# A gated mix of softmax attention and linear attention on one core: four score banks for the exponentials, part of the feature softmax on GpSimd, 482 tiles on VectorE

## The chip, the core and the metric

The kernel runs on one core of a Trainium2 chip. A core has five engines, each with its own instruction queue that is worked strictly in order: TensorE (PE, with its weight loads shown as PEld), VectorE (DVE), ScalarE (ACT), GpSimd (POOL) and SyncE (SP, which here only starts DMAs). They share the on-chip memory SBUF (128 partitions). TensorE writes its products to PSUM, eight banks of 128 x 512 float32, which VectorE and ScalarE read. The engines wait for one another by semaphores.

The metric is the device time of one execution in microseconds (us). The kernel before takes 772.43 us in the median of 3 runs (772.12 to 772.61).

## The reference

There are 2048 tokens of width 512, 32 heads of 16. Branch A is softmax attention; branch B is linear attention whose features are two softmaxes over 16 numbers each; a sigmoid gate per token mixes the two. Both branches read the same `x`.

```
scores = einsum("bhqd,bhkd->bhqk", q, k) * (Dh ** -0.5)      # A: 32 heads x 2048 x 2048
o = einsum("bhqk,bhkd->bhqd", softmax(scores), v) ... @ wo
pq = einsum("bhsd,hdf->bhsf", q, w_phi); pk likewise          # B
phi = concatenate([softmax(p), softmax(-p)], axis=-1)         # for pq and for pk
kv = einsum("bhsf,bhsd->bhfd", phi_k, v);  z = einsum("bhsf->bhf", phi_k)
o = einsum("bhqf,bhfd->bhqd", phi_q, kv) / (einsum("bhqf,bhf->bhq", phi_q, z) + 1e-6) ... @ wo
out = g * a + (1 - g) * b
```

## The kernel before

**Tiles.** Branch A is cut into 2048 tiles ("units") of 128 keys x 512 queries for one head: four units with the same keys and queries and four different heads make a pack, 16 packs make a group (4 heads, 512 queries, all 2048 keys), and there are 32 groups, so 512 packs. A unit's scores are one TensorE matmul of 32 contraction rows (`_scores`, L931); the four strips of 32 rows of the array can work side by side, and the strip of unit u is u modulo 4. A unit's exponentials are made in one of two ways.

- On ScalarE: 1596 units. Their scores go into a ring of five PSUM banks (`NRING`), in groups of alternately three and two units (`GROUPS`). One TensorE step `qk` (`_qk`) writes a group, one ScalarE instruction (`_exp`, L978) reads it and writes bfloat16 exponentials into a ring of 25 SBUF slots (`ET`, `NSLOT`). Step `qk` k waits for exponential k-2, since that one frees its banks, and must be done when exponential k-1 ends if ScalarE is not to wait.
- On VectorE: 452 units, `NUMS` of them in each group, spread evenly. `_vector_batch` takes four at a time: each unit's scores (`vqk`) go into a bank of the pool, VectorE turns them into the bits of a bfloat16 number (`v_bits`, L847), and two instructions a batch add constants to the bits (`v_step`, L864, of 2048 and 4096 elements); the four tiles that come of it are summed by TensorE into the same accumulator (`pvx`).

TensorE then multiplies with the values (`_values`, L1034), four column strips side by side: one step `pv` a pack for ScalarE's units and `pvx` steps for VectorE's. A group gathers in one PSUM bank (4 x 17 rows: 16 values and the sum). `_norm` ends a group: a transpose on VectorE (L1055), the reciprocal of the sums, the product (L1067, on POOL) and, once for two groups, a transpose back on VectorE (L1072, `n_back`), which yields `onTA`.

**PSUM.** Banks 0 to 4 are the ring. Banks 5 to 7 are a pool (`free_banks`) for the accumulators, the `vqk` scores, all projections, and branch B.

**Branch B.** `_b_fuse` multiplies `w_phi` into the projection weights once (L1128, copied out by VectorE at L1133). Then, for 8 pairs of token tiles of keys and later 8 pairs of queries, `_b_pair` projects, copies out of PSUM (L1160), negates (L1179), takes the maximum as a tree (L1181, L1182), subtracts (L1184), takes the exponential on ScalarE (L1187, 128 x 2048), sums as a tree (L1189, L1190, L1192), takes the reciprocal (L1200) and multiplies (L1194): both softmaxes at once, all but the exponential on VectorE. Keys meet the values in `_b_kv` (L1211) and are summed on VectorE. A query tile is transposed by a DMA (L1243, `phiT`), multiplied (`_b_num`, L1260), normalized on VectorE (L1266 to L1270), transposed by a DMA (L1276) and projected together with branch A in `_out`.

**The order.** Nothing on the engines is in the order in which the code is written. `Plan.order` plays the whole kernel through with a cost for every operation and writes down each engine's order; the engines then follow it with semaphores. Due times count in packs (`QDUE`, `K0`, `SK`, `Q0`, `SQ`, `NDUE`). `_late` refuses a TensorE operation that by the planner's costs would make the next `qk` late. Where TensorE has room, the planner puts in products with zeros (`_fill`, L1041) or idle products (L950). A `vqk` may be placed beside a `qk` that leaves its strip free (`_beside`).

The lines that the text below uses most, with `_qk` and `_exp`:

```
NRING = 5
GROUPS = (3, 2)
deps=self.qks[-1:] + ([self.exps[k - 2]] if k >= 2 else ...
self.ET[:, a % NS:a % NS + n, cols], self.ps[:, a % NR:a % NR + n, cols], ACT.Exp, scale=SCALE
```

## Time and profile before

The profiled execution took 772.22 us; the span from its first to its last instruction is 770.2 us, and the granted TensorE clock was 1.0.

| engine | busy, us | share of the span |
|---|---|---|
| PE | 747.0 | 97% |
| ACT | 755.1 | 98% |
| DVE | 725.3 | 94% |
| POOL | 57.9 | 8% |

Busy time is the union of the records of an engine. The record of an instruction reaches from its start to the end of its last write, and the next one of the same engine can start before that: two records in a row overlap by about 0.2 us on ScalarE and by about 0.08 us on VectorE. So an engine can show no idle time and still start its next instruction late; the distance from start to start tells that. A group of the profile is a line of the code, an engine, an operation and a shape, with its count, its busy sum, the mean of one and the idle time before it.

### The profile page before, as it was taken

The page shows a single profiled execution, that of the slowest core. Times are in us where ns is not written, and L with a number is a line of the kernel's source. Part 1 is how long each engine was busy: PE and PEld are TensorE (multiplying, and loading weights), DVE is VectorE, ACT ScalarE, POOL GpSimd, SP SyncE. Part 2 cuts the span into 40 slices and gives each one's busy share as a digit, 9 for nine tenths or more (in the row PEclk, how much of TensorE's full clock was granted, in tenths as well). Part 3 has the DMA queues.
Part 4 walks back from the last instruction along what each step waited for, and adds up shares of the span by engine and source line. Part 5 has one row for each costly group of instructions (what it writes and reads, how often), then busy time and mean ns, then how long its engine had stood idle before and what let it go on. Part 6 is the DMA issues. An engine that isn't in the chain of part 4 may idle for free.

```text
span 770.2 us, 16369 instructions
## 1 busy us (share of the span) xinstructions
PE 747.0 (97%) x7126; PEld 231.5 (30%) x7126; DVE 725.3 (94%) x1207; ACT 755.1 (98%) x663; POOL 57.9 (8%) x73
## 2 busy tenths in 40 slices
PE   8999999999999999999999999999999999999998
PEld 4333333322322232222232223222323232322222
DVE  4789999999999999999999999999999999999994
ACT  6999999999999999999999999999999999999996
POOL 3200102000010100001001010000010101010000
PEclk9999999999999999999999999999999999999999
DMA  9510000000000000000111010102001110100000
GB/s 233 124 29 1 2 1 2 1 1 2 1 1 2 1 2 1 1 2 1 29 28 29 21 35 15 42 9 49 8 9 36 32 31 16 35 9 2 1 2 28
DMA packets 46456, 16.79 MB, mean 22 GB/s; under 512 B 40752, under 2 KB 45872, under 8 KB 46384
## 3 DMA queue, kind: packets, MB, share of 16 engines
q1 hardware_dynamic: 44512, 14.97, 9.1%
q8 instruction: 55, 0.90, 0.5%
q10 hardware_dynamic: 1872, 0.79, 0.4%
q14 instruction: 17, 0.14, 0.1%
HBM read 4.21 MB, written 2.10 MB: 8 GB/s over the span
## 4 chain that ended last, share of the span: by engine, by line
ACT 87%; PE 7%; DVE 5%; DMA 1%; SPq 0%; issue 0%
ACT ET L978 83%; ACT bq L1187 4%; PE ps L931 2%; PE ps L1034 2%; PE ps L640 2%; DVE vs L847 2%; DVE vs L864 1%; DMA xT<-in_A_x_dram 1%; DVE WB L1133 0%; DVE bq L1184 0%; PE ps L1041 0%; DVE bq L1160 0%; DVE btree L1182 0%; PE ps L749 0%; DVE ghB L802 0%; SPq L515 0%
## 5 line engine op out<-in xcount | busy, mean ns | idle before, releaser
L978 ACT ACTIVATE ET<-ps 128x1024 bf16<-128x1024 f32 (+2 forms) x641 | 725.7, 1340 | 2.4 <-PE ps L931 2.4
L931 PE MATMUL ps<-qT,kT 32*128 32x512 bf16 (+1 forms) x2053 | 304.9, 383 | 12.8 <-ACT ET L978 8.2
L847 DVE TENSOR_SCALAR vs<-ps 128x512 uint16<-128x512 f32 x452 | 297.4, 681 | 13.6 <-PE ps L931 11.9
L864 DVE TENSOR_SCALAR vs<-vs 128x2048 uint16<-128x2048 uint16 x226 | 214.8, 955 | 0.8
L1034 PE MATMUL ps<-ET,V 128*32 128x512 bf16 x1596 | 196.7, 387 | 0.1
L1034 PE MATMUL ps<-vs,V 128*32 128x512 bf16 x1808 | 179.9, 384 | 2.9 <-DVE vs L864 2.7
L931 PEld LDWEIGHTS ps<-qT,kT 32*128 32x128 bf16 x2053 | 76.9, 91 | 261.0 <-ACT ET L978 187.1
L1034 PEld LDWEIGHTS ps<-ET,V 128*32 128x32 bf16 x1596 | 49.9, 94 | 92.6 <-issue 79.7
L1041 PE MATMUL ps<-kT,zero 128*32 128x512 bf16 x760 | 75.1, 383 | 0.0
L1034 PEld LDWEIGHTS ps<-vs,V 128*32 128x32 bf16 x1808 | 45.1, 95 | 67.7 <-issue 31.3
L640 PE MATMUL ps<-WB,xT 128*128 128x512 bf16 x192 | 56.7, 384 | 0.4 <-DVE WB L1133 0.4
L728 POOL TENSOR_SCALAR qT<-qtmp,mask 128x512 bf16<-128x512 bf16 x30 | 25.6, 865 | 311.2 <-DVE qtmp L723 311.2
L1067 POOL TENSOR_TENSOR T<-T,rinv 128x512 bf16<-128x512 f32 x15 | 16.5, 1102 | 296.7 <-DVE rinv L1064 296.7
L640 PE MATMUL ps<-xT,WA 128*128 128x512 bf16 x120 | 35.8, 384 | 0.0
L1187 ACT ACTIVATE bq<-bq 128x2048 bf16<-128x2048 bf16 x16 | 31.5, 1970 | 0.4 <-DVE bq L1184 0.3
L1055 DVE STREAM_TRANSPOSE T<-ps 128x512 f32<-128x512 f32 x32 | 22.7, 710 | 7.7 <-PE ps L1034 7.2
L1041 PEld LDWEIGHTS ps<-kT,zero 128*32 128x32 bf16 x760 | 19.4, 95 | 18.9 <-issue 13.7
L1160 DVE CAST bq<-ps 128x512 bf16<-128x512 f32 x32 | 21.7, 683 | 2.2 <-PE ps L640 2.2
L640 PEld LDWEIGHTS ps<-WB,xT 128*128 128x128 bf16 x192 | 14.1, 97 | 27.3 <-issue 16.4
L1184 DVE TENSOR_TENSOR bq<-bq,btree 128x2048 bf16<-128x2048 bf16 x16 | 19.8, 1240 | 0.1
L1194 DVE TENSOR_TENSOR bq<-bq,brec 128x2048 bf16<-128x2048 bf16 x16 | 19.6, 1224 | 0.0
L640 PE MATMUL ps<-WoA,onTA 128*128 128x512 bf16 x64 | 18.7, 382 | 0.0
(75 smaller groups left out, 341.2 us busy)
## 6 DMA issues: line engine op xcount, KB each, us to landing
WB<-in_B_wqkv_dram SPq DMA_DIRECT2D x1, 1536.0 KB, 8.7
out_dram<-WB SPq DMA_DIRECT2D x12, 128.0 KB, 1.7
WA<-in_A_wqkv_dram SPq DMA_DIRECT2D x2, 384.0 KB, 4.5
WoB<-in_B_wo_dram SPq DMA_DIRECT2D x1, 512.0 KB, 3.8
WoA<-in_A_wo_dram SPq DMA_DIRECT2D x1, 512.0 KB, 4.8
WA<-in_A_wqkv_dram ACTq DMA_DIRECT2D x2, 128.0 KB, 3.0
WA<-in_A_wqkv_dram ACTq DMA_DIRECT2D x1, 256.0 KB, 4.2
WA<-in_A_wqkv_dram SPq DMA_DIRECT2D x1, 256.0 KB, 5.0
```

The source lines that it names most:

```text
L640: return e.matmul(out, lhs, rhs, start=start, stop=stop)
L728: x = self.plan.op("POOL", lambda e, side=side: e.tensor_scalar(self.qT[:, s0 + side, :], tmp, self.mask[:, side:side + 1], 0.0, op0=ALU.m ...
L847: parts.append(op("DVE", lambda e, j=j, job=job: e.tensor_scalar(va[:, 0, j, :], self._bank(job), SCALE * LOG2E * 128.0, float(ORIGIN), op ...
L864: o = op("DVE", lambda e, k=k, src=src, dst=dst: e.tensor_scalar(dst, src, float(STEPS[k - 1]), None, op0=ALU.add), 0.16 + k * n * QCH * 0 ...
L931: return e.matmul(out[:, cols], self.kT[32 * i:32 * i + 32, cp, kt * TOK:(kt + 1) * TOK], self.qT[32 * i:32 * i + 32, s, cols], start=True ...
L978: o = plan.op("ACT", lambda e: e.activation(self.ET[:, a % NS:a % NS + n, cols], self.ps[:, a % NR:a % NR + n, cols], ACT.Exp, scale=SCALE ...
L1034: ins = e.matmul(self._bank(ot)[32 * i:32 * i + 32, :], v[:, v0:v0 + 32], tile, start=(kt == 0), stop=(kt == self.NT - 1), tile_position=( ...
L1041: ins = e.matmul(self._bank(ot)[32 * i:32 * i + 32, :], self.zero[:], self.kT[:, 0, 0:QCH], start=False, stop=False, tile_position=(0, 32 ...
L1055: t1 = op("DVE", lambda e: e.transpose(T1[:, side].rearrange("p b s -> p (b s)"), src()), 0.735, deps=last, writes=[b_T1[side]], name="n_t ...
L1160: [lambda e, b, k=k: e.tensor_copy(bq[:, k].rearrange("p (g s v) -> p g s v", g=8, s=2)[:, :, 0, :], b.rearrange("p (g v) -> p g v", g=8))],
L1184: + [("b_sub", two(2048), lambda e: e.tensor_tensor(x, x, spread(tree[:, :, 0]), ALU.subtract))],
L1187: op("ACT", lambda e: e.activation(flat, flat, ACT.Exp), 1.8, reads=[b], writes=[b], name="b_exp", prio=due + 1)
```

## The change

- The score ring has four banks and every group two units (`NRING = 4`, `GROUPS = (2, 2)`); the pool has four banks. The exponentials go into 22 slots. `NUMS` adds up to 482, so 1566 units stay on ScalarE.
- Branch B no longer normalizes both softmaxes. With S+ and S- the two sums of a head, only the second softmax's exponentials are multiplied, by S+/S- (`_b_ratio`), so that both carry the factor S+. For keys the factor 1/S+ goes to the values and to the columns of ones beside them, now four a block (`_b_v`, 68 columns where 65 were); for queries it cancels in the quotient, and the 1e-6 is multiplied by S+ (`r_eps`, `m_den`).
- Moved to POOL: the negation, the two smaller sums of the tree, the last sum, and the reciprocal, which becomes seven instructions on 128 elements: a guess from the bits and two Newton steps (`_reciprocal`).
- The transpose back of branch A (`n_back`) becomes DMAs for all but the last pair of groups: 16 small ones that reorder blocks into `T3` (`mix`), and one that transposes (`back`).
- The weights of `w_phi` are permuted as they stream into TensorE, so that the copy at L1133 is a plain one.
- The planner's costs, latencies, priorities and due times are other numbers, `_late` also guards the end of the kernel, and the last three `pv` go first. `PAIRS`, `P_M`, `P_REC` and `P_BMUL` are 0: the code under them is not used. So the order of nearly all instructions differs.

```diff
-        if k < 2 or k >= len(self.qks) or any(d.end is None for d in self.qks[k].deps):
+        if k >= len(self.qks) > 0:
+            x = self.exps[-1]
+            if self.last.end is not None or x.end is None and self.exps[-2].end is None:
+                return False
+            done = self.exps[-2].end + x.cost if x.end is None else x.end
+            return end > done + self.LAT["ACT"] + self.MORE["ACT", "PE"] - self.SWITCH + self.TAIL
+        if k < 2 or any(d.end is None for d in self.qks[k].deps):
...
-    NEAR = 0.2
-    SAME = 16
-    OPEN = 99
...
+    TAIL = 9.0
+    NEAR = 0.05
+    SAME = 100
+    OPEN = 2
+    HURRY, FREE = 20, 20
...
-    NRING = 5
-    GROUPS = (3, 2)
-    NSLOT = 25
+    NRING = 4
+    GROUPS = (2, 2)
+    NSLOT = 22
...
-    NA, NST, LEAD = 2, 2, 8
+    NA, NST, LEAD = 2, 2, 7
...
-    URGENT, AHEAD, SOON, REST = 5, -(1 << 30), 4, 6
-    QDUE, KDUE, VDUE = 24, 17, 8
-    P_Q, P_MUL, P_NEG = 1, 1, 0
...
+    URGENT, AHEAD, SOON, REST = 4, -(1 << 30), 4, 6
+    QDUE, KDUE, VDUE = 24, 17, 11
+    P_Q, P_MUL, P_NEG = 1, 1, 1
+    P_REC, P_SUM = 0, 4
+    P_BACK, RATIO, BV = 1, 1, 8
+    P_M, P_BMUL, CHUNKS = 0, 0, 2
     GDUE = 26
...
-    VMIN = 12
-    ALONE, EARLY = 9, 8
-    PVP = 8
...
+    VMIN = 8
+    FAST = 3
+    VSOON = -2
+    PADK = 8
+    LAST, FIRST_OUT, NEXT_OUT, DEP_OUT = 0, 8, 0, 2
+    ALONE, EARLY = 12, 6
+    PVP = 10
...
-    NUMS = (4, 10, 12, 14, 14, 14, 14, 14, 14, 14, 14, 14, 15, 14, 16, 14, 13, 14, 15, 14, 17, 14, 15, 15, 14, 14, 11, 15, 21, 16, 21, 12)
+    NUMS = (6, 10, 12, 14, 14, 16, 13, 15, 14, 17, 16, 13, 17, 15, 19, 16, 11, 18, 14, 17, 19, 14, 17, 14, 15, 20, 14, 20, 12, 16, 20, 14)
...
+        plan.last = o
+        if p >= self.NPACK - self.FAST:
+            o.prio = -1000
...
-        if side == 1:
+        if side == 1 and not alone and self.P_BACK:
+            self.b_T3.readers = self.b_T3.readers or list(self.b_wphi.readers)
+            parts = [lambda e, i=i, c=c: e.dma_start(
+                self.T3[32 * c:32 * c + 32, :, 32 * i:32 * i + 32],
+                T2[32 * i:32 * i + 32].rearrange("p (b c) f -> p c b f", c=4)[:, c]) for i in range(4) for c in range(4)]
+            self.dma("SP", f"mix{due}", parts, cost=11.0, reads=[b_T2], writes=[self.b_T3], prio=due, lat=1.5)
+            self.dma("SP", f"back{due}", lambda e: e.dma_start(dst.rearrange("p (b t) -> p b t", b=4),
+                                                               self.T3[:].rearrange("p b f -> p (b f)"), transpose=True),
+                     cost=1.3, reads=[self.b_T3], writes=[b_dst], prio=due, lat=1.7)
+        elif side == 1:
...
-    NDUE = 26
-    K0, SK, Q0, SQ = 34.0, 12.0, 214.0, 14.25
+    NDUE = 23
+    K0, SK, Q0, SQ = 30.0, 11.5, 214.0, 15.25
...
+            if self.RATIO:
+                slot = self._b_pair(1, t, due)
+                for k in range(2):
+                    self._b_v(t + k, due + self.BV + k)
+                self._b_kv(t, slot, due + self.BV + 7)
+                continue
...
-                                   self.wphi[:, cp, :], start=True, stop=True)
+                                   self.wphi[:, cp, :].rearrange("p (g i f) -> p g f i", g=2, i=4), start=True, stop=True)
...
-                self.WB[:, c, D * s:D * s + D].rearrange("p (g f i) -> p g i f", g=8, i=4),
-                self._bank(job).rearrange("p (g i f) -> p g i f", g=8, i=4)), 1.19, deps=[m],
+                self.WB[:, c, D * s:D * s + D], self._bank(job)), self.c_dve(512), deps=[m],
...
-        if t < 4:
-            self.b_VB[t].writers = [self.o_vbones]
+        at = self.VB[:, t % 4]
+        b = self.b_VB[t % 4]
+        if self.RATIO:
+            r = self.recs[:].rearrange("p (t g s i) -> p t g s i", t=2, g=8, s=2)[:, t % 2, :, 0, :]
+            ones = self.plan.op("POOL", lambda e: e.tensor_scalar(at[:, :, 64:68], r, 1.0, 0.0, op0=ALU.mult, op1=ALU.add),
+                                0.2, reads=[self.b_tree], deps=list(b.readers) + [self.o_vbones], name="r_col", prio=due)
+            evac = lambda e, bank: e.tensor_tensor(
+                at[:, :, 0:64].rearrange("p g (i d) -> p g i d", i=4), bank.rearrange("p (g i d) -> p g i d", g=8, i=4),
+                r[:, :, :, None].to_broadcast([P, 8, 4, DH]), ALU.mult)
+        else:
+            ones, evac = self.o_vbones, lambda e, bank: e.tensor_copy(at[:, :, 0:64], bank.rearrange("p (g v) -> p g v", g=8))
         self._proj(lambda c: self.xT[:, c, TOK * t:TOK * t + TOK], lambda c: self.WB[:, c, 2 * D:3 * D],
-                   [self.b_xT[t // 4], self.b_WB],
-                   [lambda e, b: e.tensor_copy(self.VB[:, t % 4, :, 0:64], b.rearrange("p (g v) -> p g v", g=8))],
-                   self.c_dve(512), due + 4, due - 3, "bv", [self.b_VB[t % 4]])
+                   [self.b_xT[t // 4], self.b_WB], [evac], self.c_dve(512), due + 4, due - 3, "bv", [b],
+                   beside=[self.b_tree] if self.RATIO else [], after=[ones] if self.RATIO else [])
+        b.writers.append(ones)
...
         chain([("b_neg", 0.16 + 1024 * 0.00027, lambda e: e.tensor_scalar(both[:, :, 1], both[:, :, 0], -1.0, 0.0,
-                                                                         op0=ALU.mult, op1=ALU.add)),
+                                                                         op0=ALU.mult, op1=ALU.add),
+                self.P_NEG * 1.1),
                ("b_max", two(1024), lambda e: e.tensor_tensor(tree, x[:, :, 0:8], x[:, :, 8:16], ALU.max))]
...
         chain([("b_sum", two(1024), lambda e: e.tensor_tensor(half, x[:, :, 0:8], x[:, :, 8:16], ALU.add))]
               + [("b_sum", two(128 * n), lambda e, n=n: e.tensor_tensor(half[:, :, 0:n], half[:, :, 0:n],
-                                                                       half[:, :, n:2 * n], ALU.add)) for n in (4, 2)]
-              + [("b_sum", 0.3, lambda e: e.tensor_tensor(last(self.bsum[:]), half[:, :, 0], half[:, :, 1], ALU.add)),
-                 ("b_rec", 0.96, self._b_rec),
-                 ("b_mul", two(2048), lambda e: e.tensor_tensor(x, x, spread(last(self.brec[:])), ALU.mult))],
+                                                                       half[:, :, n:2 * n], ALU.add),
+                  (n <= self.P_SUM) * (0.13 + 0.25 * n)) for n in (4, 2)]
+              + [("b_total", 0.3, lambda e: e.tensor_tensor(last(self.bsum[:]), half[:, :, 0], half[:, :, 1], ALU.add),
+                  (self.P_SUM > 0) * 0.38)],
               2, [b, self.b_tree])
+        if self.RATIO:
+            self._b_ratio(b, x, s, t0, due + 2)
+            return slot
...
+    def _b_ratio(self, b, x, s, t0, due):
+
+        do = lambda name, cost, fn, eng="POOL", **k: self.plan.op(eng, fn, cost, name=name, prio=due, **k)
+        halves = lambda a: a.rearrange("p (t g s i) -> p (t g) s i", t=2, g=8, s=2)
+        plus = halves(self.bsum[:])[:, :, 0, :]
+        both = [b, self.b_tree]
+        ratio = self.brec[:, 0:64].rearrange("p (g i) -> p g i", i=4)
+        self._reciprocal(self.bsum[:], self.guess[:], self.newton, self.recs[:], [self.b_guess[0]], both, due)
+        do("r_mul", 0.29, lambda e: e.tensor_tensor(ratio, plus, halves(self.recs[:])[:, :, 1, :], ALU.mult), writes=both)
...
+                do("r_eps", 0.22, lambda e, k=k, t=t: e.tensor_scalar(
+                    self.eps[:, t % 4].rearrange("p (g i) -> p g i", i=4), plus[:, 8 * k:8 * k + 8], 1e-6,
+                    self.ghB[:, t:t + 1], op0=ALU.mult, op1=ALU.mult), reads=both + [self.b_gB],
+                   writes=[self.b_eps[t % 4]])
+        y = x.rearrange("p (g s) f i -> p g s f i", s=2)[:, :, 1]
+        n = 16 // self.CHUNKS if self.P_BMUL > s else 16
+        done = []
+        for a in range(0, 16, n):
+            do("b_mul", 0.17 + 0.00188 * 64 * n if n < 16 else 0.16 + 1024 * 0.000522, lambda e, a=a: e.tensor_tensor(
+                y[:, a:a + n], y[:, a:a + n], ratio[:, a:a + n, None, :].to_broadcast([P, n, DH, 4]), ALU.mult),
+               "POOL" if n < 16 else "DVE", writes=both)
+
+    def _reciprocal(self, s, guess, tmp, out, reads, bufs, prio):
+
+        n = s.shape[-1]
+        high = lambda a: a.bitcast(U16).rearrange("p (n two) -> p n two", two=2)[:, :, 1]
+        t, r = tmp[:, 0, 0:n], tmp[:, 1, 0:n]
+        do = lambda name, cost, fn: self.plan.op("POOL", fn, cost, reads=reads, writes=bufs, name=name, prio=prio)
+        do("r_bits", 0.17 + 0.001 * n, lambda e: e.tensor_scalar(
+            high(guess), high(s), -1.0, float(0x7EE0), op0=ALU.mult, op1=ALU.add))
+        for x, y, by, plus in ((guess, r, -1.2011100358638287, 2.192845599791731), (r, out, -1.0, 2.0)):
+            do("r_mul", 0.17 + 0.0019 * n, lambda e, x=x: e.tensor_tensor(t, s, x, ALU.mult))
+            do("r_rest", 0.17 + 0.001 * n, lambda e, by=by, plus=plus: e.tensor_scalar(
+                t, t, by, plus, op0=ALU.mult, op1=ALU.add))
+            do("r_step", 0.17 + 0.0019 * n, lambda e, x=x, y=y: e.tensor_tensor(y, x, t, ALU.mult))
 
...
-            d = op("DVE", lambda e, view=view, r=r: e.tensor_scalar(
-                r, view()[:, :, 16], 1e-6, self.ghB[:, t:t + 1], op0=ALU.add, op1=ALU.mult), 0.22, reads=[self.b_gB],
-                deps=[m] + was, name="m_den", prio=due - 20)
+            if self.RATIO:
+                d = op("DVE", lambda e, view=view, r=r, hf=hf: e.scalar_tensor_tensor(
+                    out=r, in0=view()[:, :, 16], scalar=self.ghB[:, t:t + 1], in1=self.eps[:, tt, 16 * hf:16 * hf + 16],
+                    op0=ALU.mult, op1=ALU.add), 0.22, reads=[self.b_gB, self.b_eps[tt]], deps=[m] + was, name="m_den",
+                    prio=due - 20)
```

More of the change, by code (lines that the diff above doesn't have):

```diff
@@ L602, in _projections @@
             if j == 0:
-                for half, banks in enumerate(((3, 4), (None, None))):
+                for half, banks in enumerate(((3, 4) if self.NRING == 5 else (3, 2), (None, None))):
                     self._proj_k0(half, banks[0])
@@ L651, in _wide_kind, with _proj @@
         return dict(kind="col", strips=range(4)) if self.COLS else {}
-    def _proj(self, lhs, rhs, reads, evac, cost, due, rel, name, writes, n=512, bank=None, urgent=1 << 30):
+    def _proj(self, lhs, rhs, reads, evac, cost, due, rel, name, writes, n=512, bank=None, urgent=1 << 30, beside=(), after=()):
         op = self.plan.op
@@ L657, in _proj @@
         mm = None
-        war = [r for b in writes for r in b.readers]
+        war = [r for b in writes for r in b.readers] + list(after)
         for c in range(4):
@@ L839, in _vector_batch, with place @@
         n, step = len(units), (units[-1] - units[0]) / 12
-        parts, war = [], list(b_va.readers)
+        parts, war, twin = [], list(b_va.readers), {}
+        pairs = min(self.PAIRS if units[0] // (4 * NT) >= self.PAIR0 else 0, n // 2)
+        def place(j):
+            a, b = twin.get(j // 2, (None, None))
+            return j ^ 1 if a is not None and a.bank > b.bank else j
         for j, u in enumerate(units):
@@ new lines, in _b_pair @@
+        self._reciprocal(self.bsum[:], self.guess[:], self.newton, self.brec[:], [self.b_guess[0]], [b, self.b_tree], due + 2)
+        r = last(self.brec[:])[:, :, None, :]
+        if self.P_BMUL > s:
+            n = 32 // self.CHUNKS
+            done = [op("POOL", lambda e, a=a: e.tensor_tensor(x[:, a:a + n], x[:, a:a + n],
+                                                              r[:, a:a + n].to_broadcast([P, n, DH, 4]), ALU.mult),
+                       0.1 + 0.00188 * 64 * n, reads=[b, self.b_tree], deps=b.writers + self.b_tree.writers, name="b_mul",
+                       prio=due + 2) for a in range(0, 32, n)]
+            b.writers, b.readers = done, []
+        else:
+            chain([("b_mul", two(2048), lambda e: e.tensor_tensor(x, x, spread(last(self.brec[:])), ALU.mult))],
+                  2, [b, self.b_tree])
@@ L1314, in _out @@
             for x in first:
-                x.prio, x.rel = due, due - (6 if not final else 8 if tt < 2 else 0)
+                x.prio, x.rel = due, due - (6 if not final else self.FIRST_OUT if tt < 2 else self.NEXT_OUT)
                 x.deps += deps
+            if final:
+                due += self.LAST
+                for x in first:
+                    x.prio = due
             m = first[-1]
```

185 lines of the change are left out of this document (130 added, 55 removed).

## The prediction

> **What bounds the kernel now.** I read the page's busy sums and its chain first, then the groups with their shapes kept apart, the stretches of the chain, and ScalarE's and TensorE's instructions in order of time.
>
> ```profile
> PE 747.0 (97%) x7126; PEld 231.5 (30%) x7126; DVE 725.3 (94%) x1207; ACT 755.1 (98%) x663; POOL 57.9 (8%) x73
> ACT 87%; PE 7%; DVE 5%; DMA 1%; SPq 0%; issue 0%
> ```
>
> The chain that ends last is ScalarE for 87% of the span. PE's 97% says little, since its records overlap. The groups:
>
> ```profile
> L978 ACT ACTIVATE ET<-ps 128x1536 bf16<-128x1536 f32 x318 | 494.5, 1555 | 0.4 <-PE ps L931 0.3
> L978 ACT ACTIVATE ET<-ps 128x1024 bf16<-128x1024 f32 x318 | 360.8, 1134 | 1.5 <-PE ps L931 1.5
> L931 PE MATMUL ps<-qT,kT 32*128 32x512 bf16 x2043 | 303.8, 384 | 12.5 <-ACT ET L978 8.2 <-DVE vs L847 1.2
> L847 DVE TENSOR_SCALAR vs<-ps 128x512 uint16<-128x512 f32 x452 | 297.4, 681 | 13.6 <-PE ps L931 11.9
> L1034 PE MATMUL ps<-ET,V 128*32 128x512 bf16 x1596 | 196.7, 387 | 0.1
> L1034 PE MATMUL ps<-vs,V 128*32 128x512 bf16 x1808 | 179.9, 384 | 2.9 <-DVE vs L864 2.7
> L864 DVE TENSOR_SCALAR vs<-vs 128x4096 uint16<-128x4096 uint16 x113 | 138.6, 1228 | 0.3
> L864 DVE TENSOR_SCALAR vs<-vs 128x2048 uint16<-128x2048 uint16 x113 | 76.7, 683 | 0.5
> L1041 PE MATMUL ps<-kT,zero 128*32 128x512 bf16 x760 | 75.1, 383 | 0.0
> L1187 ACT ACTIVATE bq<-bq 128x2048 bf16<-128x2048 bf16 x16 | 31.5, 1970 | 0.4 <-DVE bq L1184 0.3
> ```
>
> Idle of 1.9 us ahead of 636 exponentials is not all the waiting: records overlap, so the starts must be read. ScalarE in order of time (start, length), from two places, and one stretch of the chain:
>
> ```profile
> 299.20 1.15 ACT L978 ACTIVATE ET<-ps 128x1024 bf16<-128x1024 f32 x1
> 300.10 2.03 ACT L1187 ACTIVATE bq<-bq 128x2048 bf16<-128x2048 bf16 x1
> ...
> 519.21 1.57 ACT L978 ACTIVATE ET<-ps 128x1536 bf16<-128x1536 f32 x1
> 520.54 2.03 ACT L1187 ACTIVATE bq<-bq 128x2048 bf16<-128x2048 bf16 x1
> ...
> 522.58 43.91 ACT ET L978 x39
> ```
>
> From start to start two tiles take 0.904 us (299.20 to 300.10, and the commonest distance in the trace), three 1.331 (519.21 to 520.54), the feature exponential 1.80. The slope is (1.331 - 0.904)/512 = 0.83 ns an element, so an instruction costs 0.05 us before its first element. Without waits those 39 (20 short, 19 long) take 43.37 us; they took 43.91. Over all starts in the trace, the excess is 7.0 us behind two-tile exponentials (312 steady ones, mean 22 ns, 58 late by 20 ns or more) and 1.9 us behind three-tile ones (mean 6 ns): 9.0 us hidden in a busy ScalarE.
>
> Where do those 7 us come from? One late start, TensorE and ScalarE in order of time:
>
> ```profile
> 536.74 3.92 ACT L978 ACTIVATE ET<-ps 128x1536 bf16<-128x1536 f32 x3
> ...
> 538.58 0.67 PE L931 MATMUL ps<-qT,kT 32*128 32x512 bf16 x5
> ...
> 539.21 9.14 ACT L978 ACTIVATE ET<-ps 128x1536 bf16<-128x1536 f32 x8
> ```
>
> From 536.74 to 539.21 is 2.47 where 2.235 were due. Score matmuls on different strips run together in 0.39 us; here five took 0.67, because a `vqk` held a strip of the three-tile group, whose last tile started 0.23 late. 28 of the 58 late starts behind two-tile exponentials are such split groups and hold 3.7 us; 30, with 3.0 us, are a `qk` behind too much other TensorE work.
>
> **The change part by part.** The sum is made against the profiled execution, 772.2 us (span 770.2 and 2.0 around it), 0.2 under the median.
>
> ScalarE's work. Before: 318 x (0.904 + 1.331) = 710.7. After: 2048 - 482 = 1566 units; four come in half-width instructions (4 x 0.48 = 1.9), 1562 in 781 pairs at 0.904 = 706.0, so 707.9 against 710.7 and the short first and last instructions' 2.9: **-5.7 us**. Thirty tiles fewer save 30 x 0.427 = 12.8; 145 more instructions give 7.3 back. This lies wholly on the path.
>
> ScalarE's waits. They cost 9.0 now. Every `qk` will have the short window of 0.904, which only each second one has now. Upper bound: 22 ns at each of 781, 17.4 us; lower: the 6 ns of the long window, 4.9 us. A two-tile group takes two strips, so a `vqk` finds a free one beside it and splits become rare; what stays are the 30 crowded ones and crumbs, 3.3 us in 312 windows, 10.6 ns. 781 x 10.6 ns = **8.3 us**. I take this since it is counted in the same window; it is -0.7 against now.
>
> TensorE. Same kind follows same kind 0.22 after; between row, column and full-width steps it is 0.31 to 0.32. A window of 0.904 holds a `qk` and two steps of one kind (0.32 + 0.22 + 0.31 = 0.85). To be placed: 512 `pv`, about 484 `pvx` (452 x 482/452 plus a last batch), and full-width work worth about 560 steps (456 of 512 columns, 128 of 256, 288 small ones of 0.03): 1556 steps in 783 windows, with room for about 100 more beside the sixteen exponentials of 1.80 (eight steps of 0.22 there instead of two). That fits at 93%, with the zero products (760 matmuls, 190 steps, 41 us) left out. Cost 0 if the `vqk` go beside; if not, below.
>
> VectorE. Off by mean durations: negation 6.6 (L1179), sums 11.2 and 4.5 (L1190, L1192), reciprocal, half the product, 15 of 16 transposes back, and L1133's plain copy (8 x (1.312 - 0.684) = 5.0):
>
> ```profile
> L1200 DVE RECIPROCAL brec<-bsum 128x128 f16<-128x128 f32 x16 | 15.1, 945 | 0.1
> L1194 DVE TENSOR_TENSOR bq<-bq,brec 128x2048 bf16<-128x2048 bf16 x16 | 19.6, 1224 | 0.0
> L1072 DVE STREAM_TRANSPOSE onTA<-T 128x512 bf16<-128x512 bf16 x16 | 11.2, 701 | 0.0
> ```
>
> 15.1 + (19.6 - 16 x 0.675) + 10.5: together 62 us. On: 30 x 0.681 + 8 x (0.683 + 1.228) = 35.7. Net -26 of 725, and the pool gains a bank. VectorE isn't the end of the chain, so I count 0; it keeps TensorE's waits on L847 and L864 (4.8 us in all) from growing.
>
> GpSimd. A pair's chain: negation 1.4 (two L728, 0.69 undisturbed), sums of 512 and 256 elements 1.1 and 0.6 and the last 0.4 (by L1067, 1.06 for 512), seven steps of about 0.3 (bounds 0.2, the 128x128 memset, and 1.06), ratio, eps or columns 0.8: 6.4 us, x16 = 102, POOL from 58 to 160 of 770. From exponential to feature it is 5.9 us where 3.8 were; pairs lie some 35 to 45 us apart, so it is covered. If not: `b_max` waits for `b_neg`, `b_mul` for the ratio, and behind them on VectorE stand `v_bits`, which free banks; and the value projection on TensorE waits for `r_col`, with `qk` behind it. Range 0 to 15 us, taken as 0, nearest to L1187's present wait of 0.3.
>
> What GpSimd costs VectorE shows in one place:
>
> ```profile
> 647.63 2.31 POOL L728 TENSOR_SCALAR qT<-qtmp,mask 128x512 bf16<-128x512 bf16 x2 [10.98 <-DVE qtmp L723]
> ...
> 648.04 2.98 DVE L864 TENSOR_SCALAR vs<-vs 128x2048 uint16<-128x2048 uint16 x3
> ```
>
> Two masks of 0.69 took 2.31, and three steps took 2.98 where 0.683 + 0.601 + 1.134 is 2.4. L864's long form is 1.22 alone and 1.46 in the mean of five that met POOL. The Trainium skill (Advanced Engine Details and Errata, VectorE Performance Modes) says GpSimd and VectorE's two-port modes block each other; the trace agrees, 1.22 against 1.46. Were all 102 us of new POOL time to meet such steps and each cost VectorE its full length, VectorE would lose 102 instead of winning 26, and would become the bound; by the row's 0.24 a meeting and with a third of the 224 new instructions (14 a pair) meeting one, it loses 18.
>
> DMA. `mix` is 16 issues on SP, 0.43 each by the weight loads at L578 (bound above: a transpose's 1.28), 7 to 20 us, then a transpose (2.4 to 3.2 to landing): some 12 us later than L1072, behind and ahead of phiT, onTB and the stores in SP's queue. Needed by `_out` 8 packs (12 us) after the last group of a block; a late one delays stores only. The last pair keeps VectorE's way: 0.
>
> Head and tail: the first exponential starts at 7.9, the last ends at 762.2, and the 8 us behind it are four transposes' worth of VectorE, the projection and the store, all kept. Slots 25 to 22 still lead by 11 exponentials, 10 us: 0.
>
> Sum: 772.2 - 5.7 - 0.7 = **766 us**. Own range 761 to 770: waits of 4.9 and of 12.
>
> **The rivals.** *TensorE becomes the bound* (slower). For it: 93% full, windows of mixed kind (0.32 + 0.32 + 0.31 = 0.95) are 0.05 late, a third step makes 1.06, 0.16 late. If one window in four is late by 0.08 on average, 783/4 x 0.08 = 15.7: **782 us**. Against: 41 us of zero products show spare time, and 197 `vqk` that now stand alone behind another score step, 0.24 each, can go beside. It decides from a mean lateness of 19 ns (18.8 x 781 = 14.7, with which the sum is 772.2). The Trainium skill (TensorEngine Tiling, Key Properties) says that a change of tiling mode drains TensorE; here 0.32 against 0.22, and 145 more groups with two changes each would be 29 us, 795 if none were covered.
>
> *GpSimd is late* (the meetings above). If `b_neg` is stretched as L728 was (0.69 to 1.65), each of 16 feature exponentials waits up to 0.95, 15 us; at two thirds 10: **776 us**. Against: 16 places only, 0.3 us of wait now.
>
> *It brings nothing*: splits go on and each window costs 22 ns, 757.5 + 17.4 = **775 us**, near no change; for it, the row as it stands.
>
> **How the numbers follow.** Chances: forecast 0.57, nothing gained 0.15 (half of it, with fewer splits, within 0.2%), TensorE 0.16, GpSimd 0.12. A measurement of this kernel tells a change from none at about 0.2%, 1.5 us. Faster 0.57, same 0.08, slower 0.07 + 0.16 + 0.12 = 0.35. The range reaches from 759, below the forecast's own, to 786, leaving out the worse half of the TensorE case and little else.
>
> **What would show it.** Right: two-tile exponentials 0.904 apart at the median, mean near 0.915, about 785 of them; hardly a `qk` of two passes; zero products far below 760; VectorE near 700 us busy, POOL near 160; L1187 waiting under 1 us in all. Wrong: L978's distance above 0.925, TensorE without zero products and `qk` late behind column steps, or L1187 behind L1184 by several us.

## The result, and the profile after

The changed kernel takes **781.64 us** in the median of 4 runs (780.35 to 783.90), the kernel before 772.45 us beside it (772.12 to 772.61): a ratio of 1.0123, with a 95% interval of 1.0099 to 1.0147. The forecast was 766 us and faster. The time lies inside the range of 759 to 786, on the wrong side of no change.

The page of the changed kernel, its busy sums, the granted clock in 40 slices of 19.5 us, and the chain that ended last:

```profile
PE 754.9 (97%) x7047; PEld 218.5 (28%) x7111; DVE 711.2 (91%) x1158; ACT 753.0 (97%) x807; POOL 208.9 (27%) x300
...
PEclk9995999999999999999999999999999999999999
...
ACT 74%; PE 19%; DVE 5%; DMA 1%; issue 1%
```

The span is 780.1 us of a profiled execution of 781.93. ScalarE's share of the chain has fallen from 87% to 74%, and TensorE's has risen from 7% to 19%. The line to see is the clock: in the fourth slice it is 5 tenths, where the kernel before had 9 (which stands for 90% or more) in all 40. The mean granted clock is 0.986, where 1 is full speed.

Its groups, with shapes kept apart (busy sum, mean ns of one, idle time before and what ended it):

```profile
L1041 ACT ACTIVATE ET<-ps 128x1024 bf16<-128x1024 f32 x781 | 723.2, 1168 | 13.0 <-PE ps L993 12.6 <-PE ps L1100 0.2
L1107 PE MATMUL ps<-kT,zero 128*32 128x512 bf16 x664 | 66.5, 384 | 0.0
L1216 PE MATMUL ps<-wphi,WT 128*128 128x128 bf16 x32 | 7.8, 394 | 0.2 <-issue 0.2
L1221 DVE CAST WB<-ps 128x512 bf16<-128x512 f32 x8 | 5.5, 690 | 1.3 <-PE ps L1216 1.2
```

and the answer of the kernel before to the third of them:

```profile
L1128 PE MATMUL ps<-wphi,WT 128*128 128x128 bf16 x32 | 3.2, 221 | 0.1
```

The exponentials are now L1041, the scores L993, the products of `w_phi` L1216 and their copy L1221. Idle time before the exponentials is 13.0 us, where the two shapes of before had 1.9 together. The 32 products of `w_phi` last 0.394 us each instead of 0.221. VectorE's copy of them has become the plain one that the forecast priced (0.690).

Where the 13.0 us lie is seen in stretches of 5 us of the changed kernel (length; busy time of PE, PEld, DVE, ACT and POOL, with the number of instructions; granted clock; DMA share; GB/s):

```profile
55.00:60.00 5.00, 4.84 (x37) 1.65 (x37) 4.57 (x7) 4.61 (x6) 0.00 (x0) 1.00 0.00 0
60.00:65.00 5.00, 5.00 (x24) 1.40 (x22) 4.15 (x6) 2.56 (x3) 0.00 (x0) 0.70 0.34 70
65.00:70.00 5.00, 4.67 (x15) 0.90 (x15) 1.17 (x2) 3.07 (x3) 0.00 (x0) 0.50 0.16 35
70.00:75.00 5.00, 5.00 (x22) 0.91 (x21) 1.67 (x3) 3.07 (x3) 0.00 (x0) 0.50 0.01 3
75.00:80.00 5.00, 4.84 (x27) 1.02 (x29) 1.59 (x3) 3.69 (x4) 0.00 (x0) 0.60 0.00 0
80.00:85.00 5.00, 5.00 (x42) 1.66 (x43) 3.18 (x5) 3.30 (x4) 0.00 (x0) 1.00 0.00 0
```

From 62 to 79 us the clock is at half, ScalarE works 3 us in 5, and PE shows as busy all the while. The order of time around the fall (start, length):

```profile
59.12 2.80 PE L1216 MATMUL ps<-wphi,WT 128*128 128x128 bf16 x12
61.85 0.52 PE L993 MATMUL ps<-qT,kT 32*128 32x512 bf16 x2
62.40 2.11 ACT L1041 ACTIVATE ET<-ps 128x1024 bf16<-128x1024 f32 x2 [1.89 <-PE ps L993]
...
70.06 1.02 ACT L1041 ACTIVATE ET<-ps 128x1024 bf16<-128x1024 f32 x1 [0.48 <-PE ps L993]
71.57 1.02 ACT L1041 ACTIVATE ET<-ps 128x1024 bf16<-128x1024 f32 x1 [0.48 <-PE ps L993]
```

Three things are to be seen. The twelve products stand 0.219 us apart ((2.80 - 0.394) / 11) and hold TensorE for 2.7 us; the next scores stand behind them, and an exponential waits 1.89 us. Right behind them the clock falls. And at half clock the exponentials come mostly 1.51 us apart instead of 0.904.

Read from the starts, as in the prediction, the waits behind two-tile exponentials add up to 24.6 us. 15.7 of these lie in the first 140 us, and 11 of them between 59 and 83 us. From 140 us on it is about 1 us in each 70 us, 12 to 15 ns a window.

### The profile page after: what moved, and what is told of

Its sections match the earlier page's. It is cut to its first block, busy times and chain, and to the rows that moved or that the text cites. A ratio compares the mean times of both kernels' runs of the same rounds, so it can differ in the third digit from the quotient of the medians.

```text
span 780.1 us, 16892 instructions
## 1 busy us (share of the span) xinstructions
PE 754.9 (97%) x7047; PEld 218.5 (28%) x7111; DVE 711.2 (91%) x1158; ACT 753.0 (97%) x807; POOL 208.9 (27%) x300
## 4 chain that ended last, share of the span: by engine, by line
ACT 74%; PE 19%; DVE 5%; DMA 1%; issue 1%
ACT ET L1041 71%; PE ps L993 6%; PE ps L1100 5%; PE ps L677 4%; ACT bq L1283 3%; PE ps L788 2%; DVE vs L900 2%; DVE vs L925 1%; PE ps L1216 1%; DMA xT<-in_A_x_dram 1%; DVE bq L1256 0%; DVE btree L1277 0%; DVE ghB L841 0%; PE ps L685 0%; PE ps L724 0%
## 5 line engine op out<-in xcount | busy, mean ns | idle before, releaser
L1041 ACT ACTIVATE ET<-ps 128x1024 bf16<-128x1024 f32 (+1 forms) x785 | 725.3, 1165 | 13.4 <-PE ps L993 13.0
L900 DVE TENSOR_SCALAR vs<-ps 128x512 uint16<-128x512 f32 x482 | 312.5, 682 | 25.0 <-PE ps L993 23.5
L993 PE MATMUL ps<-qT,kT 32*128 32x512 bf16 (+1 forms) x2052 | 317.2, 387 | 10.9 <-ACT ET L1041 5.9
L925 DVE TENSOR_SCALAR vs<-vs 128x2048 uint16<-128x2048 uint16 (+2 forms) x242 | 233.8, 976 | 1.2
L1100 PE MATMUL ps<-vs,V 128*32 128x512 bf16 x1928 | 211.3, 385 | 0.6 <-DVE vs L925 0.3
L1100 PE MATMUL ps<-ET,V 128*32 128x512 bf16 x1566 | 196.6, 390 | 0.3 <-DVE vs L900 0.2
L993 PEld LDWEIGHTS ps<-qT,kT 32*128 32x128 bf16 x2052 | 77.7, 91 | 317.7 <-ACT ET L1041 291.5
L1286 POOL TENSOR_TENSOR btree<-btree 128x512 f16<-128x512 f16 (+1 forms) x32 | 37.7, 1180 | 187.5 <-DVE btree L1285 186.5
L1100 PEld LDWEIGHTS ps<-ET,V 128*32 128x32 bf16 x1566 | 49.1, 94 | 82.4 <-issue 73.5
L1107 PE MATMUL ps<-kT,zero 128*32 128x512 bf16 x664 | 66.5, 384 | 0.0
L1100 PEld LDWEIGHTS ps<-vs,V 128*32 128x32 bf16 x1928 | 48.2, 95 | 51.2 <-issue 31.1
L1274 POOL TENSOR_SCALAR bq<-bq 128x1024 bf16<-128x1024 bf16 x16 | 20.3, 1266 | 138.3 <-DVE bq L1256 94.5
L677 PE MATMUL ps<-WB,xT 128*128 128x512 bf16 x169 | 51.9, 383 | 2.7 <-issue 2.2
L1283 ACT ACTIVATE bq<-bq 128x2048 bf16<-128x2048 bf16 x16 | 32.9, 2056 | 0.0
L805 POOL TENSOR_SCALAR V<-V 128x544 bf16<-128x544 bf16 x16 | 12.7, 793 | 30.3 <-DVE V L798 30.1
L1280 DVE TENSOR_TENSOR bq<-bq,btree 128x2048 bf16<-128x2048 bf16 x16 | 19.5, 1220 | 0.1
```

Source lines behind the costliest of these rows:

```text
L677: return e.matmul(out, lhs, rhs, start=start, stop=stop)
L900: bits = lambda e, to, src: e.tensor_scalar(to, src, SCALE * LOG2E * 128.0, float(ORIGIN), op0=ALU.mult, op1=ALU.add)
L925: o = op("DVE", lambda e, k=k, src=src, dst=dst: e.tensor_scalar(dst, src, float(STEPS[k - 1]), None, op0=ALU.add), 0.16 + k * n * QCH * 0 ...
L993: return e.matmul(out[:, cols], self.kT[32 * i:32 * i + 32, cp, kt * TOK:(kt + 1) * TOK], self.qT[32 * i:32 * i + 32, s, cols], start=True ...
L1041: o = plan.op("ACT", lambda e: e.activation(self.ET[:, a % NS:a % NS + n, cols], self.ps[:, a % NR:a % NR + n, cols], ACT.Exp, scale=SCALE ...
L1100: ins = e.matmul(self._bank(ot)[32 * i:32 * i + 32, :], v[:, v0:v0 + 32], tile, start=(kt == 0), stop=(kt == self.NT - 1), tile_position=( ...
```

## The experiments

The theory, formed from this trace: the loss is the permuted operand of L1216 alone. It acts in two ways: the products hold TensorE, and while they stream slowly the array is so empty that the clock is halved. Rivals: the new GpSimd work and the crowded windows of TensorE, as in the prediction; and, within the theory, that the hold alone is the loss and the clock only goes with it. "Waits" below are always the excess of the starts behind two-tile exponentials, which is 24.6 us in the changed kernel.

**1. The operand alone taken back.** The changed kernel in its own order of instructions, the products reading `w_phi` as it is stored, the permutation back in VectorE's copy.

```diff
-  self.wphi[:, cp, :].rearrange("p (g i f) -> p g f i", g=2, i=4), start=True, stop=True)
+  self.wphi[:, cp, :], start=True, stop=True)
...
-  self.WB[:, c, D * s:D * s + D], self._bank(job)), self.c_dve(512), deps=[m],
+  self.WB[:, c, D * s:D * s + D].rearrange("p (g f i) -> p g i f", g=8, i=4),
+  self._bank(job).rearrange("p (g i f) -> p g i f", g=8, i=4)), self.c_dve(512), deps=[m],
```

> The changed kernel, every engine's order kept, with only the products of w_phi as they were before: the moving operand in its stored order, the permutation back in VectorE's copy. Theory A (the permuted operand makes 32 small products four times as long, holds up score steps at 57 to 62 us and lets the clock fall to half for 17 us): those products 0.22 us long again, no half clock near 60 us, granted clock 0.995 or more, 766 to 770 us. Theory B (four banks and two-tile windows leave TensorE too little room, the clock only follows): still within 3 us of 781.6. Theory C (GpSimd's new work is late): also within 3 us of 781.6.

Measured: 771.75 us (10 runs), ratio 0.9987 (0.9978 to 0.9997). Ten of the 781.6 us are gone with one operand, while all GpSimd work and the ring of four stay. The groups of this kernel:

```profile
L1041 ACT ACTIVATE ET<-ps 128x1024 bf16<-128x1024 f32 x781 | 721.8, 1171 | 3.3 <-PE ps L993 2.7 <-PE ps L1100 0.2
L1221 DVE CAST WB<-ps 128x512 bf16<-128x512 f32 x8 | 9.8, 1303 | 0.0
L1216 PE MATMUL ps<-wphi,WT 128*128 128x128 bf16 x32 | 3.0, 221 | 0.4 <-issue 0.2
```

The waits are 14.0 us, and no slice shows half a clock. VectorE's copy is 1.30 again where the order was planned for a plain one, which may be why the time is 1.8 us above the expected range. So the operand is the cause. How much of the loss is hold and how much is clock, this run doesn't say.

**2. Held as long, with the array full.** The kernel of experiment 1 with each product issued four times into the same place.

```diff
-                for cp in range(4):
+                for cp in [x for x in range(4) for _ in range(4)]:
```

> As the run with the plain order, but each of the 32 small products of w_phi is issued four times, so that TensorE is held as long as by the permuted operand, with the array streaming all the while. A1 (the clock falls since the slow products leave the array nearly empty): no half clock near 60 us, 768 to 773 us, 3 us above the plain order at most. A2 (the clock falls since score steps are late and TensorE then waits for ScalarE): half clock near 60 us again, 778 to 784. Theories B and C: 779 to 784.

Measured: 773.29 us (10 runs), ratio 1.0015 (1.0004 to 1.0026), 0.3 above the range of A1 and 4.7 below that of A2; the waits are 16.5 us. Stretches of this kernel, in the columns of above:

```profile
55.00:60.00 5.00, 5.00 (x77) 3.84 (x75) 4.58 (x6) 3.43 (x4) 0.00 (x0) 1.00 0.01 3
60.00:65.00 5.00, 4.75 (x34) 1.47 (x33) 4.96 (x7) 4.33 (x5) 0.00 (x0) 1.00 0.51 105
65.00:70.00 5.00, 5.00 (x43) 1.24 (x41) 2.47 (x5) 5.00 (x7) 0.00 (x0) 1.00 0.00 0
```

TensorE is held as long as by the permuted operand, an exponential behind the products waits as long (1.94 us late at 60.7 us), and the clock stays full. So the hold alone does not bring the clock down; it takes the slow streaming. What is left to the changed kernel is 8.3 us.

**3. The operand alone put into the kernel before.** The kernel before in its own order, with the permuted operand and the plain copy.

> The kernel before, every engine's order kept, with only the permuted operand of the change (and the plain copy behind it). Theory A in its strong form: the products take 0.39 us, the clock falls to half between 45 and 65 us and the time is 780 to 786. In a weak form (here the 8 steps stand singly, 44 to 63 us, so the array stays busy around them): clock 1.0 and 774 to 777, the 5 us of added TensorE time partly covered. Theories B and C: 772 to 773, no effect.

Measured: 778.20 us (4 runs, 776.80 to 779.84), ratio 1.0074 (1.0054 to 1.0095), between the two forms expected. ScalarE's largest wait in this kernel and two of its stretches:

```profile
ACT ET L978 <- PE ps L931: 8.0, 15, 1.5
```

```profile
65.00:70.00 5.00, 4.67 (x27) 1.44 (x28) 3.01 (x6) 3.58 (x3) 0.00 (x0) 0.77 0.00 0
70.00:75.00 5.00, 5.00 (x19) 0.86 (x17) 1.54 (x4) 3.77 (x5) 0.00 (x0) 0.55 0.00 0
```

The clock falls here too, for 6.8 us from 67.7 on, without a ring of four and without GpSimd's new work. The four runs part by it: two with a mean clock of 0.996 took 779.5 and 779.8 us, two with 1.0 took 776.8 and 776.9. So even where the clock holds, the operand costs 4.6 us in this order (776.85 against 772.27 of the kernel before beside it). Alone it makes the old kernel slower, though it saves VectorE 4.2 us (9.7 to 5.5 in its copies).

**4. The planner told the true duration.** In the changed kernel the four products of a step are one operation of 4 x 0.22 us for the planner, and the order is made anew.

> The changed kernel with the permuted operand kept, but with 0.22 us a product in the planner's costs instead of 0.056, so that it places other work and the score steps around them by their true length; the whole order differs. Theory A: the score steps near 60 us are on time again, clock 0.995 or more, 767 to 772 us. Theories B and C: 778 to 784.

Measured: 807.42 us (4 runs), ratio 1.0454 (1.0421 to 1.0486), and not what the theory expected. The source view of L1216 (minimum, median, maximum of the length in ns, then first and last start) and the largest wait of this kernel:

```profile
L1216 PE MATMUL ps<-wphi,WT x32: 377/397/397, 162.1 to 183.0; 128*128 128x128 bf16 x32
```

```profile
ACT bq L1283 <- DVE bq L1280: 33.9, 2, 18.1
```

In the changed kernel the products start at 56.8 us, here at 162.1. A step of 0.88 us nearly fills a window of 0.904, so `_late`, as I read it, refuses it behind one score step after the other; when it comes at last, two feature exponentials wait 33.9 us together for their features, on the path, and the clock falls three times between 163 and 205 us. A true price in the planner was worse than a wrong one, since it was the price of a step too large to place.

**5. The same price in four steps.** As 4, but each product is an operation of its own of 0.22 us.

> The permuted operand is kept, with its true 0.22 us in the planner's costs, but each of the 32 products is a step of its own instead of four in one of 0.88. The order differs. If the run with the true cost was slow because a step of 0.88 fits no window of 0.904 beside a score step, so that the planner put it off to 162 us and ScalarE waited for the features: products between 54 and 100 us again, no wait of ScalarE on L1283's line above 2 us, clock 0.99 or more, 768 to 780 us (the order as a whole is another, untuned). If it was slow for another reason: above 790 us.

Measured: 784.72 us (4 runs), ratio 1.0151 (1.0131 to 1.0172), above the 768 to 780 expected. The products come from 55.4 to 105.5 us and the wait for L1280 is gone, so the reading of experiment 4 holds. The profiled execution, of 781.24 us, has a mean clock of 1.0; the three others had 0.991 to 0.993 and took 784.57 to 786.32 us. The new order also brought waits of its own, the two largest new ones of which on ScalarE are the gate's and one at the values:

```profile
ACT gh L833 <- DVE gh L830: 7.4, 1, 7.4
...
ACT ET L1041 <- PE ps L1100: 5.3, 1, 5.3
```

An order made with one number changed is another order. These two runs therefore say nothing on the operand's own price; the runs in a kept order do.

**6. Permuted once, by GpSimd.** The changed kernel in its order of instructions, with four small copies on GpSimd that write the permuted `w_phi` into a tile of its own; the products read that as it is stored, and VectorE's copy stays plain.

```diff
+        self.wphi2 = sb("wphi2", [P, 4, P], BF16)
+    def _permute(self, e):
+        for c in range(4):
+            ins = e.tensor_scalar(self.wphi2[:, c, :].rearrange("p (g f i) -> p g f i", g=2, i=4),
+                self.wphi[:, c, :].rearrange("p (g i f) -> p g f i", g=2, i=4), 1.0, 0.0, op0=ALU.mult, op1=ALU.add)
...
-  self.wphi[:, cp, :].rearrange("p (g i f) -> p g f i", g=2, i=4), start=True, stop=True)
+  self.wphi2[:, cp, :], start=True, stop=True)
```

> The changed kernel, every engine's order kept, but w_phi is permuted once, by four small GpSimd copies into a second tile at the start; the 32 products read it in stored order and VectorE's copy out stays the plain one, so that every step is as long as the planner has it. Theory A (the permuted operand is the whole loss, and the plain-order run still paid for VectorE's longer copies between 57 and 97 us): products 0.22 us long, clock 0.998 or more, ScalarE's waits near 10 us, 765 to 769 us, which is the forecast. Theory D (what the plain-order run still lost comes from elsewhere, GpSimd or the four banks): 770 to 773.

Measured: **768.20 us** in the median of 12 runs, ratio 0.9959 (0.9941 to 0.9976): faster than both kernels, and within the 765 to 769 of the theory. Nine of the runs lie between 767.84 and 769.91 us. Two took 773.95 and 774.07 with a mean clock of 0.991, and one 932.86 with 0.655, which the ratio leaves out (768.16 is the median without it); no trace of these three was kept, and their cause is open. The groups of this kernel:

```profile
L1041 ACT ACTIVATE ET<-ps 128x1024 bf16<-128x1024 f32 x781 | 720.9, 1177 | 1.6 <-PE ps L993 1.3 <-PE ps L1100 0.2
L1227 DVE CAST WB<-ps 128x512 bf16<-128x512 f32 x8 | 5.2, 678 | 0.0
L1222 PE MATMUL ps<-wphi,WT 128*128 128x128 bf16 x32 | 2.6, 220 | 0.2 <-issue 0.2
L1209 POOL TENSOR_SCALAR wphi<-wphi 128x128 bf16<-128x128 bf16 x4 | 1.5, 417 | 0.7 <-DMA wphi<-in_B_w_phi_dram 0.7
```

and its products in order of time:

```profile
56.70 0.84 PE L1222 MATMUL ps<-wphi,WT 128*128 128x128 bf16 x12
```

Twelve products take 0.84 us, 0.056 apart ((0.84 - 0.22) / 11), a quarter of the 0.219. The permutation costs GpSimd 1.5 us, once, at 28.4 us, and GpSimd has nothing else to do for 2.3 us behind it. In the profiled execution the clock is full throughout, and the waits are 11.5 us. Its chain shows 75% for ScalarE and 18% for TensorE, about as the changed kernel's, so the shift from 87% and 7% was not the loss. The 3.6 us by which this kernel is below experiment 1 go with VectorE's copy, which is plain here.

**7. Permuted once, and held all the same.** The kernel of experiment 6 with each product issued four times, as in 2.

> The kernel with w_phi permuted once into its own tile (768.2 us), with each of its 32 small products of w_phi issued four times into the same place, so that each holds TensorE about as long as the permuted operand did while the array goes on streaming. Same order of instructions, VectorE's plain copy kept. Theory (the clock falls because the array streams too little while the permuted operand is read, and the fall is the larger part of the loss): only the hold is paid, 769 to 773 us, granted clock 1.0 near 60 us, the waits within the exponentials' starts some 2 to 4 us more than the 11.5 us of the kernel with the permuted tile; what is left to the 781.6 us of the changed kernel, 9 to 12 us, is the half clock alone. Rival (the time for which TensorE is held is the loss, whatever the array does): 778 to 783 us.

Measured: 773.63 us (10 runs), ratio 1.0021 (1.0011 to 1.0031), 0.6 above the expected range and 4.4 below the rival's. A stretch of this kernel, and two rows of its order of time, one of PE's and one of ScalarE's:

```profile
55.00:60.00 5.00, 5.00 (x78) 3.88 (x75) 4.23 (x6) 3.11 (x4) 0.00 (x0) 1.00 0.01 3
...
57.13 2.85 PE L1222 MATMUL ps<-wphi,WT 128*128 128x128 bf16 x48
...
60.35 6.52 ACT L1041 ACTIVATE ET<-ps 128x1024 bf16<-128x1024 f32 x7 [1.82 <-PE ps L993]
```

The hold is 2.85 us, as in experiment 2, and the exponential behind it waits nearly as it did (1.82 us); the clock stays full, and seven exponentials follow without a pause, where the changed kernel's stood 1.5 us apart. The waits are 16.9 us, 5.4 more than in experiment 6, and the time is 5.4 us more. This takes the loss apart in one order of instructions: 768.2 without it, + 5.4 for the hold, + 8.0 for the half clock and what goes with it, 781.6.

**8. The ring of four alone.** The kernel before with four banks, groups of two and 24 slots, still 452 tiles on VectorE; a projection at the start moves from bank 4, which is gone, to bank 2.

```diff
-    NRING = 5
-    GROUPS = (3, 2)
-    NSLOT = 25
+    NRING = 4
+    GROUPS = (2, 2)
+    NSLOT = 24
```

> The kernel before with the ring of four banks and groups of two alone (24 slots; 452 tiles, VectorE and GpSimd as before); the order differs. ScalarE's own work: 796 x 0.904 + 1.9 = 721.5 against 713.6, so +7.9 us. If two-tile windows are late by about 10 ns each, as the forecast had it (waits 8 us): 778 to 782. If each is late by 22 ns as the two-tile windows of the kernel before (17 us): 786 to 790. If TensorE has no room (theory B): above 790, or a lower clock.

Measured: 785.81 us (4 runs), ratio 1.0171 (1.0157 to 1.0184), 13.4 us more, between what the two theories expected. By the prediction's own prices the work grows by 796 x 0.904 + 1.9 - 713.6 = 7.9 us; the waits grow from 9.0 to 15.7, 20 ns a window. One of them is a clock again, from 310.8 us for 3.4 us, and here TensorE had been idle for half of the 5 us ahead of it:

```profile
305.00:310.00 5.00, 2.44 (x27) 0.73 (x26) 5.00 (x8) 4.90 (x5) 0.00 (x0) 1.00 0.00 0
310.00:315.00 5.00, 5.00 (x45) 1.02 (x42) 4.11 (x7) 4.01 (x5) 0.00 (x0) 0.66 0.00 0
```

**9. The thirty tiles given back.** The kernel of experiment 6 with `NUMS` of the kernel before (452).

> As the run with w_phi permuted once, with the tile counts of the kernel before (452 instead of 482 on VectorE); the order differs. Thirty tiles more on ScalarE are 15 instructions of 0.904, 13.6 us. If ScalarE is the bound throughout: 12 to 16 us above the run with w_phi permuted once, 778 to 784. If TensorE bounds (theory B: fewer pvx steps and more zero products make room): less than 8 us above it.

Measured: 786.69 us (4 runs), ratio 1.0181 (1.0160 to 1.0202), 18.5 us more than with 482 tiles; 12 to 16 were expected. Two of its stretches:

```profile
305.00:310.00 5.00, 4.06 (x14) 0.85 (x14) 4.28 (x6) 3.71 (x4) 3.90 (x5) 0.69 0.00 0
310.00:315.00 5.00, 5.00 (x32) 0.88 (x31) 1.89 (x3) 3.21 (x4) 4.15 (x8) 0.50 0.08 8
```

The work of 30 tiles is 30 x 0.904 / 2 = 13.6 us on ScalarE, and the waits are 4.6 us more (16.1). Of these 16.1, 5.2 lie between 303 and 319 us: TensorE stood idle for 2.3 us up to 305.9, and from 306.9 to 317.1 the clock was at half. So what went beyond the tiles' work is about the size of that fall. Against experiment 8 (785.8) the rest of the change, the new feature softmax above all, shows no gain as long as VectorE gets no more tiles: its use is the time that it leaves VectorE for them. How a ring of five with 482 tiles would do was not tried.

## Why the prediction was wrong

The step that failed is the one on L1133's plain copy, "8 x (1.312 - 0.684) = 5.0", taken together with TensorE's "288 small ones of 0.03" and "Cost 0". The prediction booked what the permuted operand gives VectorE, and left the 32 products at the price of any small matmul, so that their cost on the path was nothing. The runs showed 13.4 us in its place (781.64 against 768.20 without the operand): 5.4 for the hold and 8.0 with the clock; no term of the prediction stood for either. The edit moves the permutation from VectorE's copy into TensorE's operand, and there it costs 0.219 us instead of 0.056 for each product: 32 x 0.163 = 5.2 us of TensorE. A stretch of 2.7 us, three windows long, was not hidden by a ring that is two groups ahead: the exponential behind it waited 1.9 us. To read it, the prediction needed the order of the operand's elements: in the new view neighbours lie 16 elements (32 bytes) apart. The Trainium skill (Advanced Engine Details and Errata, SBUF Cachelines) says that reads which hit another 16-byte line with each access pay for it. The traces agree, by a factor of four (0.219 against 0.056). No row of the kernel before showed such an operand on TensorE, so it should have been given bounds, as every unseen price.

Point by point:

- **ScalarE's work, -5.7: right.** 781 two-tile exponentials, 0.904 apart at the median; the first of them starts 0.7 us later than before (8.6) and the stretch behind the last is 0.6 longer (8.6).
- **ScalarE's waits, 8.3 us: wrong in the changed kernel, 24.6; nearly right without the operand, 11.5** (experiment 6: 15.1 ns in the mean, 10.6 forecast). The 2.2 us by which experiment 6 stands above the forecast's 766 are within this term's 3.2.
- **TensorE, "Cost 0 if the `vqk` go beside": right for the steady windows, wrong for one place.** From 140 us on the waits are 1 us in 70. The zero products are 664, "far below 760" was too much said: TensorE kept more room than thought.
- **The TensorE rival, 782 us, came out at the right number by another mechanism.** It put a mean lateness of 20 ns over all windows; the loss sits in one stretch some 25 us long. That the measured time agrees is luck and says nothing for it.
- **GpSimd late, 776 us: fell.** POOL was busy 208.9 us, not 160 (its instructions of 128 elements took 0.48 to 0.72 us each, taken as 0.3), and yet L1283 waited 0.0 us for its features, and the kernel of experiment 6 has the same POOL work in 768.2 us.
- **VectorE, "near 700", was 711**: in the changed kernel its step of 2048 elements took 0.714 in the mean and the one of 4096 took 1.244, against 0.683 and 1.228. The meetings with GpSimd are there, and small in sum (121 x 0.031 + 120 x 0.016 = 5.7 us): the 37 steps of 2048 elements that ran beside a GpSimd instruction took 0.780 in the mean, the 84 others 0.686; of the long ones 41 took 1.294 and 79 took 1.218.
- **"It brings nothing", 775 us: fell too**, by experiment 6. The DMA step, counted 0, has no share in the chain; the idle time of the exponentials that L1100 ended, where too few slots would show, is 0.2 us.

The chance of slower was 0.35, all of it on mechanisms that did not happen. That the range held the time is luck: a rival of about the same price stood in it.

## What to carry to other kernels

An edit that takes a permutation out of one engine's copy has put it elsewhere: find where the elements are now read in another order, and price that instruction, even where it is 32 of 7000. On an engine that feeds the bound in windows of 0.9 us, the length of the longest single step counts, not its share of the sum. And if a time is longer by more than the waits' own causes explain, look at the granted clock before the engines: here slow streaming cost more through the clock than through its own length. The same data laid out once by an idle engine (1.5 us of GpSimd) kept both gains, VectorE's plain copy and TensorE's short products.

## What the runs showed of the hardware

- **A matmul whose moving operand is read with a step of 16 elements streams four times as slowly**: 0.219 us against 0.056 from start to start for 128 columns, 0.394 against 0.221 for the record of one.
- **The clock fell with TensorE busy by its records.** In the 2.80 us of the twelve products PE shows no pause, but at the 0.056 us that such a product takes unpermuted the array had work for only 12 x 0.056 = 0.67 us of it, a quarter; right behind it the clock went to half. With 48 products in 2.85 us (experiments 2 and 7) it stayed full. The Trainium skill (TensorE: Matmul & The Clock Gate, What's actually happening) ties the half clock to an idle window of about 3.4 us. The length agrees: the falls in these traces lasted 3.4, 6.8, 10.2, 13.7 and 17.1 us, which are one to five times 3.413. The idleness agrees in experiments 8 and 9, and doesn't in the changed kernel, where it is the emptiness of the array, not a gap in the instructions, that the runs point to.
- **What share was too little.** Cut the ten traces that have clock records into stretches of 3.413 us in step with their falls, and count 0.215 us for a matmul of 512 columns (the distance from start to start), in proportion for fewer, and what overlaps once. Eight falls come before the last exponential of their trace. In the stretch ahead of each, matmuls filled 0.10 to 0.45 (0.33 ahead of the long fall, 0.45 ahead of the one at 10.8 us). Of the 2200 other stretches at full clock, two show so little (0.33 and 0.43), and the one with the 48 products of experiment 7 shows 0.88. These shares are a little low, since some matmuls have no record. The planner already puts in products with zeros where it finds less than 0.44 (`FLOOR`) of 3.3 us (`SPAN`) filled; but it counts by its own costs, and twelve products of 0.056 in a row looked like a full array to it. No run varied this share alone.
- **A fall outlasted its cause.** The slow products had ended at 61.92 us and the next came at 79.50, yet the clock stayed at half for five stretches of 3.41 us. The exponentials came mostly 1.51 us apart, since scores and two more steps now took that long. What ended it is open.
- **It varies by execution.** The changed kernel's four runs had a mean clock of 0.989, 0.987, 0.986 and 0.983 at 780.35, 781.35, 781.93 and 783.90 us. In the profiled one there was a second fall, from 10.8 to 14.2 us, far ahead of the products, with some 1.3 us of waits at it; no run here shows why it came in this execution. The long one by itself gives 0.989 (17.1 / 2 / 778.6 = 0.011), so the execution of 780.35 us seems to have had no other.
